# Attention with a pooled branch and top-128 routing: all stages placed anew in program order, pooling of q and k split over GpSimd and VectorE

## The chip, the cores and the metric

One core of one Trainium2 chip runs the whole program. The metric is device time in microseconds for one execution, the median of several runs. The engines are named as in the profile: PE is TensorE's matmul side and PEld its weight load, DVE is VectorE, ACT is ScalarE, POOL is GpSimd, and SP is the engine that only issues DMAs here.

## The reference, cut to what matters

Inputs are q, k and v with 8 batches, 8 heads, 576 rows and 64 columns. Two attentions are added. The coarse one averages q, k and v over groups of 4 rows (144 rows are left), does a full softmax attention on them, and repeats each result row 4 times. The local one is a softmax attention in which row i sees only the keys with |i - j| < 4. Their sum, with the heads side by side, is x (576 x 512 for each batch). Then a routed layer changes 128 rows of each batch:

```python
scores = np.einsum('bsd,d->bs', x, w_gate)
out = x.copy()
for b in range(B):
    top_idx = np.argpartition(-scores[b], capacity)[:capacity]   # capacity = 128
    xe = x[b, top_idx]
    h = np.maximum(xe @ w1, 0.0)                                  # w1 512 x 1024
    ye = h @ w2                                                   # w2 1024 x 512
    g = 1.0 / (1.0 + np.exp(-scores[b, top_idx]))
    out[b, top_idx] = x[b, top_idx] + g[:, None] * ye
```

## The kernel before, in words

All 8 batches are written out one after the other, and each is cut into generators ("stages"), whose steps are sorted by a position and run in that order to write the program. For batch b the stages are:

- QK (`load_qk`): two DMAs of 1152 KB from ACT's queue load q and k transposed into `T`, half of the head pairs each. Two buffers.
- PL (`pool_qk`): sums groups of 4 columns of `T` into `dT`, in four VectorE reductions of 128x1152 elements to 128x288 (L55 in the profile, where all DMAs and VectorE operations that go through the helper `InOrder` have that line). Two small ACT copies into `qz` follow.
- VP (`pool_v`): one DMA of 1152 KB loads `vraw`; three GpSimd additions of 128x576 make `vd` (L199, L201), and one multiplication makes `vr` (L205).
- VW (`load_vw`): three DMAs load windows of v for the local attention, with one buffer each (`vw0` to `vw2`).
- Two coarse units: scores `sd` (L229, L236), their maxima, exponentials `ed` (ACT, L254), transposes, and the products `od` (L295 to L308). Then ACT copies `odr` (L316), VectorE makes `ods` (L317), and SP issues DMAs that spread these rows four-fold into the tiles `x` (`raise_rows`, "x<-ods").
- Three local units (`sl`, `ex`, `pspl`, `pt`, `ol`, `t`) cover the five 116-row tiles; the first two units have two tiles each, the last has one. VectorE writes each tile's result `t` (L415).
- XS (`sums`), three steps: GpSimd adds `x = x + t` (L428), VectorE multiplies with the gate and sums into the score (`jk`, L430), SP writes `x` out.
- RT (`route`), 15 events: scores are compared all with all (`sb` L453, `srow` L455, five `beat` operations L466), the ranks give a one-hot matrix `oh`, a matmul `pi` (L487) gives the indices `idx` (L491). GpSimd issues the gather of the chosen rows (L498, `xe`). After six empty steps PE transposes them (`px`, L506), and ACT and VectorE split them into two fp16 parts (`xeh`, `xel`).
- MO (`moe`), 16 events: matmuls `ph` (L526 to L530) and `py` (L543 to L545), the final `xe` (L548), and GpSimd's scatter (L549).

Batch b's main units fill the position b to b + 1, in the proportions `WU`, each with three phases `PH`. Every other stage has a start and a span in `PLACE` against a base: b - 1 for QK, VP, VW and PL, b for XS, b + 1 for RT and MO; step i of n stands at base + start + span * (i + 0.5) / n. A last event also runs whatever steps its stage has left. Weights (WT) and constants (CS) are placed in the same way.

The sorted steps give the program's order. Three kinds of instructions keep that order strictly among themselves on their engine: DMAs and conversions on ACT called through `aq`, all of SP's DMAs, and the VectorE operations called through `vq` (pooling and weight conversion). For the rest the framework may let an instruction of the same engine pass ahead of one that is not ready by its own estimate. On the chip each engine runs its instructions strictly in the order it was given.

Of the kernel before, what the change touches and what calls it, by code (L numbers as in the profile page):

```python
# [11 lines left out]
F32 = mybir.dt.float32  # L12
# [4 lines left out]
ALU = mybir.AluOpType  # L17
AX = mybir.AxisListType
# [3 lines left out]
P = 128  # L22
# [11 lines left out]
XS = 16.0  # L34
WS = 64.0


PH = (-0.9, 0.2, 0.6)
WU = (2.2, 2.6, 5.2, 5.2, 2.6)
PLACE = {  # L40
# [4 lines left out]
}  # L45


# [11 lines left out]
def tile_multires_attention_moe(ctx: ExitStack, tc: tile.TileContext, qk, vw, vp, cs, w_gate, w1, w2, outs):  # L59


    nc = tc.nc
    B, _, _, HP, S = qk.shape
    pool = nc.gpsimd
    sp, aq, vq = (InOrder(tc, e) for e in (nc.sync, nc.scalar, nc.vector))
    D = P // 2
    H = 2 * HP
    DM = H * D
# [15 lines left out]
    ld = ctx.enter_context(tc.tile_pool(name="ld", bufs=2))  # L84
    wk = ctx.enter_context(tc.tile_pool(name="wk", bufs=2))
# [84 lines left out]
    def pool_qk(b):  # L170
        qkdT[b] = wk.tile([P, 2, HP, SD], F32, tag="dT", name=f"dT{b}")
        T, dT, hh = qkT[b], qkdT[b], HP // 2
        Tv = T.rearrange("p n h (c r) -> p n h c r", r=FACTOR)
        for u in range(2):
            hs = slice(hh * u, hh * (u + 1))
            for n in range(2):
                vq.tensor_reduce(out=dT[:, n, hs], in_=Tv[:, n, hs], axis=AX.X, op=ALU.add)
                yield
        qz = qzbuf[b % 2]
        for a in range(2):  # L180
            nc.scalar.copy(qz[64 * a : 64 * a + 64, :, a, :], dT[64 * a : 64 * a + 64, 0, :, P:])
        yield
# [158 lines left out]
    ts = [[] for _ in range(B)]  # L341
# [83 lines left out]
    def sums(b):  # L425
        for x, tiles in zip(xs, TU):
            for i, j in enumerate(tiles):
                pool.tensor_tensor(out=x[:, i], in0=x[:, i], in1=ts[b][j], op=ALU.add)  # L428
                jk = wk.tile([P, DM], F32, tag="jk", name="jk", bufs=1)
                nc.vector.scalar_tensor_tensor(  # L430
                    out=jk, in0=x[:, i], scalar=1.0, in1=wg, op0=ALU.mult, op1=ALU.mult,
                    accum_out=scs[b][:, j : j + 1],
                )
            for e in range(2):
                n = qns[2 * tiles[-1] + e]
                for p0, p1 in ((0, 48), (48, n)):
                    xv = bass.AP(
                        tensor=x_d[b].tensor, offset=x_d[b][2 * QB * tiles[0] + QB * e + p0, 0:1].offset,
                        ap=[[DM, p1 - p0], [2 * QB * DM, len(tiles)], [1, DM]],
                    )  # L440
                    sp.dma_start(out=xv, in_=x[64 * e + p0 : 64 * e + p1])
            yield


    def route(b, sc):
        va = vals[b % 2]
        scp = sm.tile([P, NT], F32, tag="scp", name="scp")
        nc.vector.tensor_tensor(out=scp, in0=sc, in1=pen, op=ALU.add)
        nc.scalar.copy(va[:, :, 1], scp)
        sb = psA.tile([P, 2, 512], F32, tag="A", name="sb")  # L450
        sbf = sb.rearrange("p a (j u) -> p (a j) u", u=P)
        for j in range(NT):
            nc.tensor.transpose(sbf[:, j], scp[:, j : j + 1].broadcast_to([P, P]), ident)  # L453
        srow = wk.tile([P, NT, P], F32, tag="srow", name="srow", bufs=2)
        nc.scalar.copy(srow, sbf[:, :NT])  # L455
        yield


        acc = sm.tile([P, NT], F32, tag="acc", name="acc")
        sr = srow.rearrange("p j u -> p (j u)")  # L460
        cb = psT.tile([P, 512], F32, tag="Q", name="cb")
        nc.tensor.matmul(cb[:, :NT], lhsT=identb, rhs=off, start=True, stop=False, skip_group_check=True)
        for j in range(NT):
            n = P * (NT - j)
            beat = wk.tile([P, NT, P], BF16, tag="beat", name="beat")
            nc.vector.scalar_tensor_tensor(  # L466
                out=beat[:, : NT - j].rearrange("p j u -> p (j u)"), in0=sr[:, P * j :],
                scalar=scp[:, j : j + 1], in1=first[:, :n], op0=ALU.subtract, op1=ALU.is_gt,
                accum_out=acc[:, j : j + 1],
            )  # L470
            for k in range(j + 1, NT):
                nc.tensor.matmul(
                    cb[:, k : k + 1], lhsT=beat[:, k - j], rhs=ones, start=False,
                    stop=j == NT - 2, skip_group_check=True,
                )
            yield
        nc.vector.scalar_tensor_tensor(
            out=acc, in0=acc, scalar=-1.0, in1=cb[:, :NT], op0=ALU.mult, op1=ALU.add
        )
        oh = wk.tile([P, NT, CAP], F32, tag="oh", name="oh", bufs=1)  # L480
        for j in range(NT):
            nc.scalar.activation(oh[:, j], iota, AF.Abs, bias=acc[:, j : j + 1])
        nc.scalar.activation(oh, oh, AF.Relu, bias=1.0, scale=-1.0)
        yield
        pi = psT.tile([P, 512], F32, tag="Q", name="pi")
        for j in range(NT):
            nc.tensor.matmul(  # L487
                pi[:, :2], lhsT=oh[:, j, :], rhs=va[:, j, :], start=j == 0, stop=j == NT - 1
            )
        idx = sm.tile([P, 1], I32, tag="idx", name="idx", bufs=3)  # L490
        nc.vector.tensor_copy(idx, pi[:, 0:1])  # L491
        gs = sm.tile([P, 1], F32, tag="gs", name="gs", bufs=3)
        nc.scalar.activation(gs, pi[:, 1:2], AF.Exp, scale=-1.0)
        nc.vector.tensor_scalar(gs, gs, 1.0, XS * WS * WS, op0=ALU.add, op1=ALU.mult)
        nc.vector.reciprocal(gs, gs)

        xe = wk.tile([P, DM], F32, tag="xe", name="xe", bufs=2)
        pool.indirect_dma_start(  # L498
            out=xe, out_offset=None, in_=x_d[b],
            in_offset=bass.IndirectOffsetOnAxis(ap=idx, axis=0),  # L500
        )
        for _ in range(6):
            yield
        px = psT.tile([P, NC, CAP], F32, tag="Q", name="px")
        for c in range(NC):
            nc.tensor.transpose(px[:, c, :], xe[:, P * c : P * (c + 1)], ident)  # L506
        xeh = wk.tile([P, NC, CAP], F16, tag="xeh", name="xeh", bufs=2)
        xel = wk.tile([P, NC, CAP], F16, tag="xel", name="xel", bufs=2)
        nc.scalar.activation(xeh, px, AF.Copy, scale=XS)  # L509
        nc.vector.scalar_tensor_tensor(  # L510
            out=xel, in0=px, scalar=XS, in1=xeh, op0=ALU.mult, op1=ALU.subtract
        )
        yield
        moes[b] = moe(b, idx, gs, xe, xeh, xel)
# [75 lines left out]

    ends = [sum(WU[:i]) / sum(WU) for i in range(len(WU) + 1)]
    nu = len(WU)
    mains = []
# [4 lines left out]
    for b in range(B):  # L598
        pq = put(lambda b=b: pool_qk(b), 5, *when("PL", b, b - 1), lqk[b])
        pv = put(lambda b=b: pool_v(b), 3, *when("VP", b, b - 1))  # L600
        lv = put(lambda b=b: load_vw(b), 3, *when("VW", b, b - 1))
        if weights is None:
            put(lambda: consts, 1, *when("CS", 0, -1))
            weights = put(load_weights, 11, *when("WT", 0, 0))
        for i in range(nu):
            need = (pq, pv) if i < 2 else ()
            g = put(lambda b=b, i=i: unit(b, i), 0, 0, 0, *need)
            e0, e1 = ends[i], ends[i + 1]
            for ph in range(3):
                events.append((b + e0 + PH[ph] * (e1 - e0), len(events), g, ph == 2))  # L610
            mains.append(g)
        xa = put(lambda b=b: sums(b), 3, *when("XS", b, b))
        rt = put(lambda b=b: route(b, scs[b]), 15, *when("RT", b, b + 1), *mains[-nu:], xa)
        put(lambda b=b: moes[b], 16, *when("MO", b, b + 1), weights, rt)
# [75 lines left out]
```

## Time and profile before

| | us |
|---|---|
| median of 3 runs | 398.24 |
| lowest, highest run | 394.81, 398.83 |
| the profiled execution | 392.69 |
| its span in the trace | 390.9 |
| mean granted TensorE clock in it | 0.847 of full speed |

All rows come from that one profiled execution, which is 1.4% shorter than the median; the 1.8 us outside its span are start and end of the program. A busy share is a mean over parts with different limits, so rows of one round (one batch's period) are read beside it. The chain of waits is followed back from the last instruction: at each step to what released it, or to the instruction before it on its engine.

### The profile page before, as it was taken

What the parts mean: (1) busy time and instruction counts of PE and PEld (TensorE: products, weight loads), DVE (VectorE), ACT (ScalarE), POOL (GpSimd) and SP (SyncE); (2) the same over time, 40 slices, a digit from 0 to 9 for tenths busy, and PEclk for the clock granted to TensorE, in tenths of its full rate; (3) what the DMA queues carried; (4) which work ended last, traced back from release to release, by engine and by line L of the source; (5) the groups of instructions that cost most, each with busy time, mean ns of one, the idle gap of its engine ahead of it and who ended that gap; (6) DMA issues with size and microseconds to landing.
All of it is one profiled execution on the core that took longest, in us unless ns stands there. A gap on an engine that the chain in (4) does not pass through costs nothing.

```text
span 390.9 us, 10860 instructions
## 1 busy us (share of the span) xinstructions
PE 297.6 (76%) x4584; PEld 224.3 (57%) x4584; DVE 250.8 (64%) x525; ACT 144.7 (37%) x385; POOL 117.9 (30%) x100
## 2 busy tenths in 40 slices
PE   0783568627999699849896699949996589985884
PEld 0553446526775686537665577637855467664471
DVE  2675978876677976565567877764675936576021
ACT  0543345623543353513534153513642144422210
POOL 3504620363008410652007510553009210251011
PEclk9996557956899899966999599966999569999599
DMA  8799877763578385845538375765567341642000
GB/s 314 284 329 291 266 224 282 209 170 61 196 270 194 90 261 197 200 147 174 198 109 229 95 251 171 216 169 150 173 231 176 87 118 29 130 104 74 27 29 27
DMA packets 24169, 67.93 MB, mean 174 GB/s; under 512 B 3608, under 2 KB 3736, under 8 KB 23096
## 3 DMA queue, kind: packets, MB, share of 16 engines
q10 hardware_dynamic: 10912, 43.55, 32.7%
q1 hardware_dynamic: 11928, 19.49, 21.3%
q0 software_dynamic: 1280, 4.20, 3.4%
q8 instruction: 36, 0.59, 0.6%
q14 instruction: 13, 0.11, 0.1%
HBM read 45.92 MB, written 11.53 MB: 147 GB/s over the span
## 4 chain that ended last, share of the span: by engine, by line
PE 32%; issue 17%; DVE 14%; POOL 13%; DMA 12%; ACT 7%; SPq 3%; POOLq 1%; ACTq 1%; DVEq 0%
POOL x L428 5%; DMA vraw<-in_vp_dram 5%; ACT ed L254 3%; POOL vd L201 3%; PE sd L229 3%; PE od L295 3%; SPq L55 3%; DVE jk L430 3%; DVE dT L55 3%; DMA x<-ods 3%; PE ph L526 3%; PE ph L529 2%; DMA out_dram<-x 2%; PE ph L530 2%; PE ol L405 2%
## 5 line engine op out<-in xcount | busy, mean ns | idle before, releaser
L428 POOL TENSOR_TENSOR x<-x,t 128x512 f32<-128x512 f32 x40 | 53.0, 1331 | 64.2 <-DVE t L415 44.1
L430 DVE SCALAR_TENSOR_TENSOR jk<-x,wg 128x512 f32<-128x512 f32 x40 | 38.9, 975 | 27.1 <-POOL x L428 25.4
L199 POOL TENSOR_TENSOR vd<-vraw 128x576 f32<-128x576 f32 x8 | 11.4, 1423 | 147.0 <-DMA vraw<-in_vp_dram 106.8
L529 PE MATMUL ph<-xel,w1h 128*128 128x128 f16 x256 | 49.9, 232 | 1.7 <-DVE xel L510 0.9
L526 PE MATMUL ph<-xeh,w1h 128*128 128x128 f16 x256 | 50.3, 233 | 0.7 <-ACT xeh L509 0.7
L530 PE MATMUL ph<-xeh,w1l 128*128 128x128 f16 x256 | 49.8, 232 | 0.0
L405 PE MATMUL ol<-vw,pt 64*64 64x65 f32 x1280 | 35.9, 257 | 17.8 <-DVE ex L383 4.6
L55 DVE TENSOR_REDUCE dT<-T 128x288 f32<-128x1152 f32 x32 | 42.8, 1343 | 4.1 <-DMA T<-in_qk_dram 4.1
L405 PEld LDWEIGHTS ol<-vw,pt 64*64 64x64 f32 x1280 | 29.3, 164 | 25.2 <-issue 13.8
L395 ACT COPY pt<-pspl 128x512 f32<-128x512 f32 x40 | 22.6, 585 | 32.6 <-PE pspl L393 32.5
L393 PE MATMUL pspl<-cst,ex 128*128 128x128 f32 x160 | 28.5, 318 | 6.9 <-ACT ex L387 6.2
L371 PE MATMUL sl<-T 64*58 64x64 f32 (+1 forms) x1280 | 32.2, 232 | 0.0
L371 PEld LDWEIGHTS sl<-T 64*58 64x58 f32 (+1 forms) x1280 | 27.8, 140 | 7.3 <-issue 5.7
L387 ACT ACTIVATE ex<-ex 128x1024 f32<-128x1024 f32 (+1 forms) x24 | 21.9, 913 | 26.5 <-DVE ex L383 26.5
L526 PEld LDWEIGHTS <-w1h 128*128 128x128 f16 x256 | 27.0, 106 | 4.1 <-issue 2.8
L415 DVE TENSOR_TENSOR t<-ol,den 128x512 f32<-128x512 f32 x40 | 27.6, 690 | 1.2
L529 PEld LDWEIGHTS <-w1h 128*128 128x128 f16 x256 | 27.0, 105 | 2.2 <-issue 1.6
L229 PE MATMUL sd<-dT 64*128 64x144 f32 x128 | 20.9, 434 | 9.5 <-DVE dT L55 7.9
L530 PEld LDWEIGHTS <-w1l 128*128 128x128 f16 x256 | 27.0, 106 | 1.6 <-issue 1.6
L380 DVE TENSOR_REDUCE mx<-sl 128x16 f32<-128x1024 f32 (+1 forms) x24 | 25.0, 1040 | 3.2 <-PE sl L371 3.2
L506 PE MATMUL px<-cst,xe 128*128 128x128 f32 x32 | 7.4, 375 | 25.2 <-DMA xe<-out_dram,idx 25.2
L254 ACT ACTIVATE ed<-sd,mxd 128x144 f32<-128x144 f32 x64 | 25.9, 525 | 0.5
(98 smaller groups left out, 604.3 us busy)
## 6 DMA issues: line engine op xcount, KB each, us to landing
T<-in_qk_dram ACTq DMA_DIRECT2D x16, 1152.0 KB
vraw<-in_vp_dram ACTq DMA_DIRECT2D x8, 1152.0 KB
vw<-in_vw_dram ACTq DMA_DIRECT2D x16, 520.0 KB
x<-ods SPq DMA_DIRECT2D x64, 120.0 KB
out_dram<-x SPq DMA_DIRECT2D x32, 192.0 KB
stg<-in_moe_w_dram ACTq DMA_DIRECT2D x8, 512.0 KB
vw<-in_vw_dram ACTq DMA_DIRECT2D x8, 260.0 KB
out_dram<-x SPq DMA_DIRECT2D x16, 96.0 KB
```

The source lines that it names most:

```text
L55: return lambda *a, **k: self.tc.keep_in_program_order(f(*a, **k))
L229: nc.tensor.matmul(s[:, a, SD * i : SD * (i + 1)], lhsT=dT[64 * a : 64 * a + 64, 0, hp, :P], rhs=dT[64 * a : 64 * a + 64, 1, hp, :], start ...
L254: nc.scalar.activation(ed[:, :, h] if h < H else er, s[:, a, SD * i : SD * (i + 1)], AF.Exp, bias=mx[:, c : c + 1], scale=pscale, accum_ou ...
L371: nc.tensor.matmul(s[64 * e : 64 * e + qn, a, c : c + KW], lhsT=T[64 * a : 64 * a + 64, 0, hp, q0s[blk] : q0s[blk] + qn], rhs=T[64 * a : 6 ...
L393: nc.tensor.transpose(ps[:, hp, :], ex[:, HP * i + hp, :], ident)
L405: nc.tensor.matmul(o[64 * e : 64 * e + 64, a, D1 * hp : D1 * (hp + 1)], lhsT=pt[64 * a : 64 * a + 64, hp, 64 * e : 64 * e + 64], rhs=vl[64 ...
L415: nc.vector.tensor_tensor(out=t.rearrange("p (g a d) -> p a g d", a=2, d=D), in0=ov[:, :, :, 0:D], in1=den.unsqueeze(3).broadcast_to([P, 2 ...
L428: pool.tensor_tensor(out=x[:, i], in0=x[:, i], in1=ts[b][j], op=ALU.add)
L430: nc.vector.scalar_tensor_tensor(out=jk, in0=x[:, i], scalar=1.0, in1=wg, op0=ALU.mult, op1=ALU.mult, accum_out=scs[b][:, j : j + 1],)
L526: nc.tensor.matmul(ph[:, i, :], lhsT=w1h[:, c, fs], rhs=xeh[:, c, :], start=c == 0, stop=False)
L529: nc.tensor.matmul(ph[:, i, :], lhsT=w1h[:, c, fs], rhs=xel[:, c, :], start=False, stop=False)
L530: nc.tensor.matmul(ph[:, i, :], lhsT=w1l[:, c, fs], rhs=xeh[:, c, :], start=False, stop=c == NC - 1)
```

## The change

Four things are changed.

1. Every number of `PH`, `WU` and `PLACE` is new, and so is the order of the program.
2. `pool_qk` does, for each half of the head pairs, one GpSimd addition of neighbouring columns (128x1152 results into a new tile `half`, two buffers, both inputs with stride 2) and, one step later, one VectorE addition of neighbouring results (128x576, both inputs with stride 2). The four reductions go.
3. In `sums`, the addition of `t` to `x` runs on VectorE for the last batch; for the others it stays on GpSimd. `jk` has two buffers.
4. `route` has eight empty steps in place of six after the gather, so that `px` falls on the stage's last event.

```diff
--- before.py
+++ after.py
@@ -35,13 +35,24 @@
 WS = 64.0
 
 
-PH = (-0.9, 0.2, 0.6)
-WU = (2.2, 2.6, 5.2, 5.2, 2.6)
+PH = (-0.9, 0.192, 0.601)
+WU = (2.19, 2.6, 5.16, 5.21, 2.548)
 PLACE = {
-    "QK": (-0.15, 0.2), "VP": (0.1, 0.7), "VW": (0.55, 0.75), "PL": (0.1, 0.7),
-    "RT": (0.0, 0.9), "MO": (0.8, 1.0), "CS": (0.6, 0.1), "XS": (0.45, 0.75), ("XS", 7): (0.3, 0.98), "WT": (0.0, 1.6),
-    ("RT", 7): (0.0, 0.5), ("MO", 5): (1.0, 0.9), ("MO", 6): (1.0, 0.5), ("MO", 7): (0.5, 0.5),
-    ("MO", 0): (1.0, 1.0),
+    "QK": (-0.164, 0.2),
+    "VP": (-0.041, 0.71),
+    "VW": (0.292, 0.507),
+    "PL": (0.084, 0.717),
+    "RT": (0.0, 0.936),
+    "MO": (0.971, 0.985),
+    "CS": (0.54, 0.212),
+    "XS": (0.472, 0.839),
+    ("XS", 7): (0.268, 1.075),
+    "WT": (-0.173, 1.567),
+    ("RT", 7): (-0.027, 0.719),
+    ("MO", 5): (0.548, 1.14),
+    ("MO", 6): (1.077, 0.52),
+    ("MO", 7): (0.988, 0.487),
+    ("MO", 0): (1.04, 0.905),
 }
 
 
@@ -173,9 +184,13 @@
         Tv = T.rearrange("p n h (c r) -> p n h c r", r=FACTOR)
         for u in range(2):
             hs = slice(hh * u, hh * (u + 1))
-            for n in range(2):
-                vq.tensor_reduce(out=dT[:, n, hs], in_=Tv[:, n, hs], axis=AX.X, op=ALU.add)
-                yield
+            hv = ld.tile([P, 2, hh, S // 2], F32, tag="half", name="half", bufs=2)
+            e2 = T.rearrange("p n h (c r) -> p n h c r", r=2)
+            pool.tensor_tensor(out=hv, in0=e2[:, :, hs, :, 0], in1=e2[:, :, hs, :, 1], op=ALU.add)
+            yield
+            h2 = hv.rearrange("p n h (c r) -> p n h c r", r=2)
+            vq.tensor_tensor(out=dT[:, :, hs], in0=h2[..., 0], in1=h2[..., 1], op=ALU.add)
+            yield
         qz = qzbuf[b % 2]
         for a in range(2):
             nc.scalar.copy(qz[64 * a : 64 * a + 64, :, a, :], dT[64 * a : 64 * a + 64, 0, :, P:])
@@ -425,8 +440,9 @@
     def sums(b):
         for x, tiles in zip(xs, TU):
             for i, j in enumerate(tiles):
-                pool.tensor_tensor(out=x[:, i], in0=x[:, i], in1=ts[b][j], op=ALU.add)
-                jk = wk.tile([P, DM], F32, tag="jk", name="jk", bufs=1)
+                last = b == B - 1
+                (nc.vector if last else pool).tensor_tensor(out=x[:, i], in0=x[:, i], in1=ts[b][j], op=ALU.add)
+                jk = wk.tile([P, DM], F32, tag="jk", name="jk", bufs=2)
                 nc.vector.scalar_tensor_tensor(
                     out=jk, in0=x[:, i], scalar=1.0, in1=wg, op0=ALU.mult, op1=ALU.mult,
                     accum_out=scs[b][:, j : j + 1],
@@ -499,7 +515,7 @@
             out=xe, out_offset=None, in_=x_d[b],
             in_offset=bass.IndirectOffsetOnAxis(ap=idx, axis=0),
         )
-        for _ in range(6):
+        for _ in range(8):
             yield
         px = psT.tile([P, NC, CAP], F32, tag="Q", name="px")
         for c in range(NC):
```

## Rows read from the trace of the kernel before

**Rows 1.** Busy time, share of the span and instruction count of each engine (the page's first part), whole span.
```profile
PE 297.6 (76%) x4584; PEld 224.3 (57%) x4584; DVE 250.8 (64%) x525; ACT 144.7 (37%) x385; POOL 117.9 (30%) x100
```

**Rows 2.** Busy time of each engine in five stretches, each from the end of one batch's `od` matmuls (L308) to the next one's (the first begins earlier, at 100.0, inside batch 2's round). Columns: start:end and length in us; busy us and instructions of PE, PEld, DVE, ACT, POOL; granted TensorE clock as a share of full speed; DMA share; GB/s. The last row has sum and mean.
```profile
100.00:152.40 52.40, 47.73 (x816) 37.41 (x811) 40.37 (x85) 23.32 (x66) 14.33 (x11) 0.96 0.65 200
152.40:200.80 48.40, 39.77 (x563) 29.32 (x562) 28.93 (x66) 17.14 (x47) 13.95 (x11) 0.86 0.56 163
200.80:241.30 40.50, 33.23 (x576) 26.28 (x574) 31.23 (x62) 16.93 (x47) 13.46 (x11) 0.87 0.65 194
241.30:286.40 45.10, 38.73 (x585) 29.07 (x583) 28.42 (x64) 17.00 (x47) 14.03 (x11) 0.85 0.60 175
286.40:330.50 44.10, 34.47 (x548) 25.96 (x546) 29.23 (x64) 16.36 (x46) 13.47 (x11) 0.81 0.47 125
sum 230.50, PE 193.93 PEld 148.04 DVE 158.18 ACT 90.75 POOL 69.24; mean PE 38.79 PEld 29.61 DVE 31.64 ACT 18.15 POOL 13.85
```

**Rows 3.** The chain that ended last over the whole span, in order of time: start us, us, what (a row with "DMA" runs from issue to landing); first its shares by line.
```profile
by line: issue 17.4%; POOL x L428 5.0%; DMA vraw<-in_vp_dram 5.0%; ACT ed L254 3.4%; POOL vd L201 3.1%; PE sd L229 3.0%; PE od L295 3.0%; SPq L55 2.9%; DVE jk L430 2.8%; DVE dT L55 2.8%; DMA x<-ods 2.7%; PE ph L526 2.6%; PE ph L529 2.4%; DM
...
1.43 8.43 DMA T<-in_qk_dram
...
25.69 8.27 DMA vraw<-in_vp_dram
...
84.99 4.47 issue
...
152.38 0.87 PE od L308 x2
153.35 5.84 DMA vraw<-in_vp_dram
...
200.83 0.87 PE od L308 x2
...
206.67 3.02 DMA x<-ods
...
217.77 4.50 issue
...
241.34 0.87 PE od L308 x2
242.31 5.53 DMA vraw<-in_vp_dram
...
286.40 0.87 PE od L308 x2
...
295.38 3.50 DMA x<-ods
...
303.33 5.48 issue
...
330.52 0.86 PE od L308 x2
```

**Rows 4.** Timeline of POOL from 195 to 345 us (batches 4 and 7): start us, us, engine, line, operation, out<-in, count, and in brackets the idle time before it and what ended that.
```profile
207.53 1.44 POOL L199 TENSOR_TENSOR vd<-vraw 128x576 f32<-128x576 f32 x1 [23.26 <-DMA vraw<-in_vp_dram]
...
211.95 0.98 POOL L498 DMA_INDIRECT xe<-out_dram,idx  x1 [0.30 <-issue]
...
214.30 2.48 POOL L428 TENSOR_TENSOR x<-x,t 128x512 f32<-128x512 f32 x2
216.73 1.04 POOL L205 TENSOR_TENSOR vr<-vd,cst 128x512 f32<-128x512 f32 x1
...
340.99 1.27 POOL L428 TENSOR_TENSOR x<-x,t 128x512 f32<-128x512 f32 x1 [1.88 <-issue]
```

**Rows 5.** Timeline of DVE from 195 to 232 us, same columns.
```profile
207.88 0.16 DVE L491 CAST idx<-pi 128x1 int32<-128x1 f32 x1 [0.17 <-PE pi L487]
...
215.60 2.73 DVE L430 SCALAR_TENSOR_TENSOR jk<-x,wg 128x512 f32<-128x512 f32 x1 [2.88 <-POOL x L428]
```

**Rows 6.** Waits between 60 and 345 us, one row: engine and line that waited, what it waited for, us in total, times, longest.
```profile
PE px L506 <- DMA xe<-out_dram,idx: 25.2, 6, 6.3
```

**Rows 7.** Timeline of PE from 205 to 226 us, same columns.
```profile
217.92 1.08 PE L506 MATMUL px<-cst,xe 128*128 128x128 f32 x4 [4.90 <-DMA xe<-out_dram,idx]
...
219.09 1.15 PE L405 MATMUL ol<-vw,pt 64*64 64x65 f32 x32
...
225.44 0.70 PE L405 MATMUL ol<-vw,pt 64*64 64x65 f32 x32
```

**Rows 8.** Groups of instructions by line and shape over the whole span: xcount | busy us, mean ns of one | idle before, with what ended it.
```profile
L428 POOL TENSOR_TENSOR x<-x,t 128x512 f32<-128x512 f32 x40 | 53.0, 1331 | 64.2 <-DVE t L415 44.1 <-DVE den L413 13.8 <-DMA out_dram<-x 4.5
...
L55 DVE TENSOR_REDUCE dT<-T 128x288 f32<-128x1152 f32 x32 | 42.8, 1343 | 4.1 <-DMA T<-in_qk_dram 4.1
L430 DVE SCALAR_TENSOR_TENSOR jk<-x,wg 128x512 f32<-128x512 f32 x40 | 38.9, 975 | 27.1 <-POOL x L428 25.4 <-DMA out_dram<-x 1.4 <-DMA x<-ods 0.3
...
L201 POOL TENSOR_TENSOR vd<-vd,vraw 128x576 f32<-128x576 f32 x16 | 24.3, 1520 | 0.9
```

**Rows 9.** Timeline of all engines from 353.2 to 356.3 us (the last tile of the last batch), same columns as the other timelines.
```profile
353.33 0.69 DVE L415 TENSOR_TENSOR t<-ol,den 128x512 f32<-128x512 f32 x1
...
354.15 1.27 POOL L428 TENSOR_TENSOR x<-x,t 128x512 f32<-128x512 f32 x1 [1.91 <-DVE t L415]
...
355.46 0.69 DVE L430 SCALAR_TENSOR_TENSOR jk<-x,wg 128x512 f32<-128x512 f32 x1 [0.84 <-POOL x L428]
```

## The prediction

> **What bounds the kernel now.** I read the busy shares first: no engine is full, PE is busy 76% of the span, DVE 64%, POOL 30% [rows 1]. So the time is made of waits between engines, and the next view is the stretches of one batch each. The chain of waits passes the end of `od` at 153.25, 201.70, 242.21, 287.26 and 331.38 us [rows 3], so a round takes (331.38 - 153.25) / 4 = 44.5 us, of which PE is busy 33 to 40, DVE 28 to 31 and POOL 14 [rows 2]. Third, the chain itself. In these rounds it runs from the end of `od` into the DMA of `vraw` (5.84 and 5.53 us, 8.27 in the first round), through POOL's three `vd` additions, the gather and the `x` additions, and then into stretches marked "issue" of 4.47, 4.50 and 5.48 us [rows 3]. The timelines explain both pieces for batch 4. `vraw` is issued from ACT's queue behind the copy of `od`, so it starts only when `od` ends; POOL sits idle for 23.26 us until it lands, and everything behind it in POOL's queue starts late: the gather at 211.95, though its indices were there at 208.04 [rows 4, 5], and the first `x` addition at 214.30, 12.6 us after `od`. PE then reaches `px` at 213.0 and stands still for 4.90 us until the gathered rows land [rows 7]. That idle time also costs clock: right after it the 32 `ol` matmuls take 1.15 us, as at 1.2 GHz, against 0.70 us later at 2.4 GHz [rows 7]; the granted clock was 0.81 to 0.87 in the four full rounds and 0.96 in the stretch before [rows 2].
>
> **The change part by part.** Positions are in rounds.
>
> *(a) VP earlier.* `vraw` moves from 0.217 to 0.077 of a round, ahead of the coarse unit's second and third phases (0.152 and 0.212), so its DMA no longer waits for `od`; its additions move from 0.45 to 0.314. The wait of [rows 4] goes. What is late next is seen in batch 7, which has no `vraw` behind it: its first `x` addition starts at 340.99, 9.6 us after `od` [rows 3, 4]; the spread rows land at 206.67 + 3.02 = 209.69, 8.0 us after `od`. Gain per round: 12.6 - 9.6 = 3.0, at least 0, at most 12.6 - 8.0 = 4.6. Six rounds: -18.0 (0 to -27.6).
>
> *(b) Gather to `px`.* The gather stands at 0.468 (before 0.45), `px` on RT's last event at 0.905 (before 0.81), so the distance grows from 0.36 to 0.437 of a round, 3.4 us more. Before, PE came to `px` 5.0 us after the indices (213.02 against 208.04) and the gather needed 217.92 - 211.95 = 6.0 us after 3.9 us of delay on POOL. After, PE comes 8.4 us behind the indices, and the gather needs 6.0, or 8.7 if it stands behind the new second GpSimd addition (0.442): a wait of 0 to 0.3 us. PE's six waits are 25.2 us in all [rows 6]; only the three "issue" pieces on the chain count, 14.5 [rows 3]. Against that, batch 5's new MO start (0.548) pulls its `px` forward to 0.116 after the gather, about 5 us, where one wait like the old ones returns (4.5). Sum -10.0 (-25.2 to +4.5).
>
> *(c) Pooling.* Removed: 32 reductions of 1.343 us, 43.0 us of DVE [rows 8]. Added on DVE: 16 additions of 576 elements. Nearest is `jk`, also two SBUF operands: 0.69 us for 512 undisturbed [rows 9], so 0.75 (up to 2.73, its longest [rows 5]); 12.0 in all. Added on POOL: 16 additions of 1152. The `x` addition takes 1.27 us for 512 undisturbed [rows 4, 9], which makes 2.9 for 1152; `vr` takes 1.04 for 512, which makes 2.3; the mean of `vd` is 1.52 for 576, which makes 3.0 [rows 4, 8]. I take 2.7 (2.3 to 3.0; stride 2 on GpSimd is in no row): 43 us, 5.4 a round on an engine that is busy 14 of 44.5. That hides them, and the DVE half is one step (0.143 round, 6.4 us) later, so it does not wait. On the chain the reductions have 2.8% of 390.9 = 10.9 us [rows 3]; shortened in the ratio 12/43 that leaves 3.0: -7.9 (0 to -10.9). The other side is a collision. A DVE operation with two SBUF operands does not run beside a POOL addition: `jk` began at 215.60 and lasted 2.73 us, until the POOL operations then running (`x` to 216.78, `vr` to 217.77) were over [rows 4, 5]. In the mean `jk` takes 0.975 against 0.69 [rows 8, 9], so 40 x 0.285 = 11.4 us are lost beside 117.9 us of POOL. POOL becomes 117.9 + 43 - 6.7 (five `x` additions gone) = 154, which makes the loss 14.9, and 16 new DVE additions are exposed by 0.285 each, 4.6: +8 on DVE, half of it on the chain: +4 (0 to 16 x 2.7 = 43). Together -3.9.
>
> The Trainium skill speaks against this part: "GPSIMD Engine Reference", § 4.1 Engine selection, sends elementwise work on a tile to VectorE and calls GpSimd about twice as slow for two inputs, and § 1 Specifications says its SBUF interfaces are shared with VectorE where that has two SBUF inputs. The 2.73 us row agrees with the second. By the first rule alone the kernel would get slower by this part; the third rival below is that case.
>
> *(d) `x` on DVE for batch 7.* Last tile: `t` ends at 354.02, `jk` begins at 355.46 after the POOL addition [rows 9], 1.44 us; DVE's own addition takes about 0.69. -0.75, and the same for the tile before: -1.5 (-2 to +2.1, if the three other additions fall on the path). The rest of the tail keeps its order: `ph` of batch 6 before the routing, `py` behind `pi`, then `px`.
>
> *(e) Start.* Earlier issue of the first round's `vraw` (8.27 us on the chain) by 0.14 round would be worth 6, but five weight loads now stand ahead of position 0.47 instead of three and share the DMA engines: -2. The price the other way: batch 0's second GpSimd addition is placed behind `vd`, so if it runs there, pooling ends 3 x 1.4 + 2.7 = 7 us later. Range -6 to +7.
>
> *Loads with one buffer.* The `vw` loads now stand before the last reader of their buffer (0.377 against 0.446 and so on), so they go out when it is free, and the next `T` loads queue behind the last of them, at about 0.95 instead of 0.90. `T` is needed at 1.156, 9 us later; a `T` load took 8.43 in the crowded start [rows 3], so 0, up to +2 a round. The second `jk` buffer changes nothing: DVE writes them in order.
>
> *The other places.* The `x` steps move from 0.575 and 0.825 to 0.612 and 0.891, with the output DMAs that SP issues for them; the last step stays at 1.03, and SP's next work, the spread of the next batch, stands at 1.21, 8 us later, so SP has time. MO moves back by 0.16 of a round, its scatter on POOL from 0.519 to 0.679, behind the first `x` additions instead of ahead of them; only the program's end waits for a scatter. These are costed at nothing; if the later `x` steps reach the spread, they cost what they moved, 0.05 round or 2 us each round.
>
> Sum: -18.0 - 10.0 - 3.9 - 1.5 - 2.0 = -35.4. PE would allow it: busy time times clock is 31.0 us a round in the four full rounds; at clock 0.96 and the 91% share of the first stretch (47.73 of 52.40) a round needs 35.5 us, below the 44.5 - 5.3 = 39.2 of the sum. But (a), (b) and (c) lie on one chain with PE, DVE and SP close behind, so I count two thirds of their 31.9: -21. With (d) and (e): -24.5, 392.7 to 368.2. The runs' median is 398.24 / 392.69 = 1.014 of the profiled execution, so 373.4; I say 373.
>
> **Rivals.**
> 1. *The whole sum.* -35.4: 357.3, in the median's measure 362. For it: the 35.5 us that PE needs. Against: rounds without a `vraw` or `px` piece on the chain are not shown.
> 2. *The next wait takes its place.* SP's spread DMAs, on the chain with 3.02 and 3.50 us just before `x`, end last anyway; then (a) and (c) are worth nothing, (b) half (-5), and (d) and (e) stay: -8.5, 384.2, so 390.
> 3. *POOL's additions become the wall.* Each of the 16 additions stops a two-operand DVE operation for its full 2.7 us and holds the gather and the `x` behind it: +43, (a) lost, (b) half: -5, reductions -7.9, (d) and (e) -3.5: +27, 420, so 425. It decides once about 10 of the 16 stops fall on the chain (24.5 / 2.7, and (a) lost with them). Against: POOL is idle 30 of 44.5 us a round, and the positions lie away from `jk`.
> 4. *The order is not what the positions say.* The framework lets ready instructions pass, and the engines' order hardly differs: within 1%, 398.
>
> **How the numbers follow.** Forecast 0.50, rivals 0.18, 0.15, 0.11 and 0.06. The forecast's own range is 365 to 385. Low end 358, below the whole sum; high end 398, which leaves out rival 3 and little else. A measurement here tells about 1% from no change (394.3 to 402.2). Faster: 0.49 + 0.18 + 0.12 = 0.79; same: 0.01 + 0.03 + 0.05 = 0.09; slower: the rest, 0.12.
>
> **What would show it.** Right: POOL's long idle before `vd` no longer ends with `vraw`'s DMA on the chain; the first `x` starts under 10 us after `od`; PE's waits at `px` fall from 25.2 us to 5; the granted clock in the rounds rises to 0.9 or more; the GpSimd additions take 2.7 us and DVE's 0.75; a round is near 41 us. Wrong: `jk` and `beat` longer in the mean than now, DVE idle ended by POOL's additions, or the chain passing through SP's spread DMAs in every round, with rounds of 44 us.

## The result: 365.0 us, and where the time went

The changed kernel takes 365.0 us (median of 4 runs, 363.12 to 375.13); the kernel before, run beside it, 397.41 (394.81 to 398.83). The ratio is 0.9176, 95% interval [0.9101, 0.9251]. The profiled execution takes 364.34 us with a span of 362.5, against 392.69 and 390.9: -28.3 us, where the prediction counted -24.5 of a sum of -35.4. Some executions of a kernel take over 1.5% longer than its fastest one; the ratios leave them out, none is given where only one execution is left (e1, e12 below), and the profiles of e1, e10 and e12 are of such executions. From L55 on, all lines stand 11 to 16 further down in the new program (L55 is L66, `od`'s end L323, `x` L444, `jk` L446, `beat` L482, gather L514, `px` L522, scatter L565).

Busy time of each engine over the span (answers [rows 1]):
```profile
PE 289.3 (80%) x4584; PEld 215.6 (59%) x4584; DVE 253.1 (70%) x514; ACT 143.1 (39%) x385; POOL 151.8 (42%) x111
```
VectorE is as busy as before, 253.1 us against 250.8, though 32 reductions of 1.34 us became 16 additions: the first surprise.

Five rounds, each from the end of one batch's `od` to the next one's; columns as in [rows 2], which this answers:
```profile
113.50:151.40 37.90, 35.22 (x613) 26.68 (x612) 30.68 (x63) 16.36 (x47) 20.23 (x15) 1.00 0.70 209
151.40:189.70 38.30, 34.59 (x575) 25.93 (x574) 30.80 (x63) 16.46 (x47) 19.73 (x14) 0.96 0.69 205
189.70:227.60 37.90, 34.45 (x576) 26.07 (x575) 30.97 (x64) 16.58 (x47) 19.46 (x14) 0.95 0.70 208
227.60:263.80 36.20, 33.21 (x576) 24.80 (x575) 27.79 (x61) 16.49 (x47) 16.95 (x12) 1.00 0.73 217
263.80:306.90 43.10, 39.01 (x573) 27.84 (x572) 27.63 (x64) 17.39 (x48) 12.67 (x11) 0.96 0.43 107
```
The first four of these are the rounds of batches 2 to 6, and they hold nearly all of the gain. In one stretch each, first before, then after:
```profile
112.40:287.30 174.90, 148.50 (x2331) 113.20 (x2334) 120.53 (x257) 68.39 (x190) 55.77 (x44) 0.88 0.61 180
```
```profile
113.50:263.80 150.30, 137.47 (x2332) 103.49 (x2331) 120.24 (x249) 65.89 (x188) 76.37 (x53) 0.98 0.71 210
```
That is -24.6 us. The rest of the span: up to the first `od` +2.5 (25.6 to 28.1), the two rounds after it -1.4, the last round -1.0, the tail behind the last `od` -3.9 (59.5 to 55.6); together -28.4. A middle round was 43.7 us, PE busy 37.1 and idle 6.6, at clock 0.88; now it is 37.6, busy 34.4 and idle 3.2, at 0.98. So a little over half of the gain is idle time of PE that went (3.4 a round), and the rest is the same matmuls (2331 and 2332) taking 2.8 us less at the higher clock.

The chain of waits, cut to one round (answers [rows 3]):
```profile
by line: issue 13.5%; DMA xe<-out_dram,idx 8.6%; SPq L66 8.1%; DVE beat L482 7.9%; DMA x<-ods 5.4%; DMA T<-in_qk_dram 4.9%; DMA vw<-in_vw_dram 3.6%; ACT ed L269 3.1%; PE ol L420 2.4%; DMA stg<-in_moe_w_dram 2.2%; DVE jk L446 1.9%; PE sl L38
...
226.76 0.86 PE od L323 x2
228.98 0.89 SPq L66
...
231.72 3.39 DMA x<-ods
235.14 6.66 DMA xe<-out_dram,idx
243.23 6.57 DMA vw<-in_vw_dram
```
`vraw` is gone from it. On the chain now are SP's spread, then the gather, which `px` waits for. POOL in that round (answers [rows 4]):
```profile
217.32 4.75 POOL L189 TENSOR_TENSOR half<-T 128x1152 f32<-128x1152 f32 x2 [5.23 <-DMA out_dram<-x]
222.78 1.41 POOL L214 TENSOR_TENSOR vd<-vraw 128x576 f32<-128x576 f32 x1 [0.70 <-DMA vraw<-in_vp_dram]
224.26 3.13 POOL L216 TENSOR_TENSOR vd<-vd,vraw 128x576 f32<-128x576 f32 x2
227.77 1.04 POOL L220 TENSOR_TENSOR vr<-vd,cst 128x512 f32<-128x512 f32 x1 [0.37 <-PE od L323]
233.73 1.27 POOL L444 TENSOR_TENSOR x<-x,t 128x512 f32<-128x512 f32 x1 [4.92 <-DMA x<-ods]
235.14 1.34 POOL L514 DMA_INDIRECT xe<-out_dram,idx  x1
```
The `vd` additions stand before the end of `od` (227.6), where they stood behind it; their wait for `vraw` falls from 23.3 us at the longest to 4.8. The first `x` starts 6.1 us after `od`; in batches 1 to 6 it starts 6.1 to 7.7 us after, against 8.6 to 12.6 before. The bracket names the spread, but in this round `x` waits for `t` as much: VectorE's `t` ends at 233.65, and `x` starts 0.08 us later.
```profile
232.96 0.69 DVE L430 TENSOR_TENSOR t<-ol,den 128x512 f32<-128x512 f32 x1
```

PE's wait at `px` (answers [rows 6]), and PE at that place (answers [rows 7]):
```profile
PE px L522 <- DMA xe<-out_dram,idx: 11.7, 6, 3.5
```
```profile
239.80 0.58 PE L420 MATMUL ol<-vw,pt 64*64 64x65 f32 x28
241.85 0.66 PE L522 MATMUL px<-cst,xe 128*128 128x128 f32 x4 [1.46 <-DMA xe<-out_dram,idx]
...
242.44 0.70 PE L420 MATMUL ol<-vw,pt 64*64 64x65 f32 x32
```
The wait is there still, in six rounds, but it is short, and the 32 `ol` behind it take 0.70 us, the speed of 2.4 GHz.

Groups by shape (answers [rows 8]), and VectorE in batch 7's last tiles (answers [rows 9]):
```profile
L446 DVE SCALAR_TENSOR_TENSOR jk<-x,wg 128x512 f32<-128x512 f32 x40 | 32.6, 817 | 16.0 <-POOL x L444 14.2 <-DMA T<-in_qk_dram 1.4 <-DMA out_dram<-x 0.3
...
L66 DVE TENSOR_TENSOR dT<-half 128x576 f32<-128x576 f32 x16 | 18.8, 1182 | 7.6 <-POOL half L189 7.6
L482 DVE SCALAR_TENSOR_TENSOR beat<-srow,scp,first 128x512 bf16<-128x512 f32 x8 | 13.3, 1664 | 0.0
...
L189 POOL TENSOR_TENSOR half<-T 128x1152 f32<-128x1152 f32 x16 | 35.7, 2252 | 45.2 <-DMA T<-in_qk_dram 35.2 <-DMA out_dram<-x 9.9
```
```profile
322.60 0.69 DVE L430 TENSOR_TENSOR t<-ol,den 128x512 f32<-128x512 f32 x1
323.33 0.69 DVE L444 TENSOR_TENSOR x<-x,t 128x512 f32<-128x512 f32 x1
324.06 0.69 DVE L446 SCALAR_TENSOR_TENSOR jk<-x,wg 128x512 f32<-128x512 f32 x1
```

### The profile page after: what moved, and what is told of

Read it like the earlier page. It is cut to its first block, busy times and chain, and to the rows that moved or that the text cites. A ratio compares the mean times of both kernels' runs of the same rounds, so it can differ in the third digit from the quotient of the medians.

```text
span 362.5 us, 10864 instructions
## 1 busy us (share of the span) xinstructions
PE 289.3 (80%) x4584; PEld 215.6 (59%) x4584; DVE 253.1 (70%) x514; ACT 143.1 (39%) x385; POOL 151.8 (42%) x111
## 4 chain that ended last, share of the span: by engine, by line
DMA 25%; PE 22%; DVE 18%; issue 13%; SPq 8%; ACT 7%; POOL 4%; ACTq 1%; POOLq 0%; DVEq 0%
DMA xe<-out_dram,idx 9%; SPq L66 8%; DVE beat L482 8%; DMA x<-ods 5%; DMA T<-in_qk_dram 5%; DMA vw<-in_vw_dram 4%; ACT ed L269 3%; PE ol L420 2%; DMA stg<-in_moe_w_dram 2%; DVE jk L446 2%; PE sl L386 2%; PE od L310 2%; DVE mxd L257 2%; PE ph L542 1%; DVE dT L66 1%
## 5 line engine op out<-in xcount | busy, mean ns | idle before, releaser
L444 POOL TENSOR_TENSOR x<-x,t 128x512 f32<-128x512 f32 x35 | 46.8, 1342 | 82.3 <-DVE t L430 40.2
L189 POOL TENSOR_TENSOR half<-T 128x1152 f32<-128x1152 f32 x16 | 35.7, 2252 | 45.2 <-DMA T<-in_qk_dram 35.2
L482 DVE SCALAR_TENSOR_TENSOR beat<-srow,scp,first 128x640 bf16<-128x640 f32 (+4 forms) x40 | 46.8, 1207 | 1.2 <-ACT srow L471 0.7
L446 DVE SCALAR_TENSOR_TENSOR jk<-x,wg 128x512 f32<-128x512 f32 x40 | 32.6, 817 | 16.0 <-POOL x L444 14.2
L420 PE MATMUL ol<-vw,pt 64*64 64x65 f32 x1280 | 29.7, 234 | 14.7 <-DVE ex L398 7.5
L420 PEld LDWEIGHTS ol<-vw,pt 64*64 64x64 f32 x1280 | 24.5, 144 | 21.5 <-issue 10.6
L386 PE MATMUL sl<-T 64*58 64x64 f32 (+1 forms) x1280 | 34.4, 230 | 0.0
L430 DVE TENSOR_TENSOR t<-ol,den 128x512 f32<-128x512 f32 x40 | 27.6, 691 | 1.3
L408 PE MATMUL pspl<-cst,ex 128*128 128x128 f32 x160 | 26.0, 300 | 1.5 <-ACT ex L402 1.5
L546 PEld LDWEIGHTS <-w1l 128*128 128x128 f16 x256 | 26.6, 104 | 0.7 <-issue 0.6
L216 POOL TENSOR_TENSOR vd<-vd,vraw 128x576 f32<-128x576 f32 x16 | 26.3, 1647 | 1.2
L514 POOL DMA_INDIRECT xe<-out_dram,idx x8 | 10.1, 1260 | 38.8 <-DVE idx L507 22.1
```

The lines of the kernel that those rows point to most:

```text
L189: pool.tensor_tensor(out=hv, in0=e2[:, :, hs, :, 0], in1=e2[:, :, hs, :, 1], op=ALU.add)
L386: nc.tensor.matmul(s[64 * e : 64 * e + qn, a, c : c + KW], lhsT=T[64 * a : 64 * a + 64, 0, hp, q0s[blk] : q0s[blk] + qn], rhs=T[64 * a : 6 ...
L420: nc.tensor.matmul(o[64 * e : 64 * e + 64, a, D1 * hp : D1 * (hp + 1)], lhsT=pt[64 * a : 64 * a + 64, hp, 64 * e : 64 * e + 64], rhs=vl[64 ...
L430: nc.vector.tensor_tensor(out=t.rearrange("p (g a d) -> p a g d", a=2, d=D), in0=ov[:, :, :, 0:D], in1=den.unsqueeze(3).broadcast_to([P, 2 ...
L444: (nc.vector if last else pool).tensor_tensor(out=x[:, i], in0=x[:, i], in1=ts[b][j], op=ALU.add)
L446: nc.vector.scalar_tensor_tensor(out=jk, in0=x[:, i], scalar=1.0, in1=wg, op0=ALU.mult, op1=ALU.mult, accum_out=scs[b][:, j : j + 1],)
```

## The experiments

Theory A: the places did it, above all VP's (`vraw` off the chain) and the longer way from gather to `px`. Rival B: the lighter VectorE did it, by the pooling. Theory C came up after the first kernels: QK's place, because it takes the `T` loads past other work on ACT's queue. Each part was undone in the new kernel, or done alone in the old one. All of them in one table; the kernel before took 395.68, 394.9 and 397.13 us beside the three groups (e1, e2, e3, e5; e10, e11, e12, e4; e13, e6, e14, e15). "Round" is the mean of the four middle rounds of the profile, as PE's busy plus idle time, from one stretch as above.

| kernel | median us | ratio [95%] | round | clock |
|---|---|---|---|---|
| the change | 365.0 | 0.9176 [0.9101, 0.9251] | 34.4 + 3.2 | 0.98 |
| e1 change, pooling undone | 361.57 | none given; 361.57/395.68 = 0.914 | 34.7 + 3.3 | 0.98 |
| e2 before + pooling | 395.09 | 0.9991 [0.9944, 1.0039] | 36.2 + 6.5 | 0.90 |
| e3 before + VP | 391.75 | 0.9874 [0.9757, 0.999] | 37.0 + 5.5 | 0.91 |
| e5 change, VP undone | 388.47 | 0.9813 [0.9731, 0.9895] | 36.0 + 6.0 | 0.93 |
| e10 change, QK undone | 363.22 | 0.9136 [0.9051, 0.9222] | 35.4 + 3.4 | 0.96 |
| e11 before + VP, QK | 376.79 | 0.9495 [0.9428, 0.9562] | 34.9 + 5.5 | 0.94 |
| e12 before + VP, QK, RT, MO | 380.37 | none given; 380.37/394.9 = 0.963 | 37.4 + 5.9 | 0.90 |
| e4 before + RT, MO | 407.35 | 1.0269 [1.0198, 1.0341] | 37.2 + 6.3 | 0.90 |
| e13 change, RT, MO undone | 380.3 | 0.9606 [0.954, 0.9672] | 35.5 + 3.8 | 0.95 |
| e6 change, `x` on GpSimd | 368.65 | 0.928 [0.9211, 0.9349] | 35.2 + 4.0 | 0.96 |
| e14 change, VW, XS undone | 361.17 | 0.9137 [0.9062, 0.9213] | 35.0 + 2.5 | 0.97 |
| e15 before + VP, QK, VW, XS | 382.91 | 0.9654 [0.9573, 0.9735] | 36.6 + 4.9 | 0.93 |

**The pooling: e1 and e2.** The changed kernel with the four reductions a batch, and the old one with the two pairs of additions.
```diff
 e1, against the changed kernel (e2 is the reverse, against the kernel before)
-            hv = ld.tile([P, 2, hh, S // 2], F32, tag="half", name="half", bufs=2)
-            e2 = T.rearrange("p n h (c r) -> p n h c r", r=2)
-            pool.tensor_tensor(out=hv, in0=e2[:, :, hs, :, 0], in1=e2[:, :, hs, :, 1], op=ALU.add)
-            yield
-            h2 = hv.rearrange("p n h (c r) -> p n h c r", r=2)
-            vq.tensor_tensor(out=dT[:, :, hs], in0=h2[..., 0], in1=h2[..., 1], op=ALU.add)
-            yield
+            for n in range(2):
+                vq.tensor_reduce(out=dT[:, n, hs], in_=Tv[:, n, hs], axis=AX.X, op=ALU.add)
+                yield
```


> The changed kernel with the four VectorE reductions of the kernel before in pool_qk, at the changed kernel's places. Theory A (the new places make the gain; the reductions saved on VectorE come back as beat and jk operations stretched beside GpSimd's additions, so pooling is worth little): 361 to 370 us, beat back from 1.21 to 0.61 us in the mean. Rival B (the gain is the 31 us less pooling work on VectorE): 380 us or more.

> The kernel before with only the new pooling (one GpSimd and one VectorE addition for each half). Theory A: 392 to 404 us, with beat and jk stretched beside GpSimd. Rival B: 383 us or less.

e1 (355.7 to 364.35 us) takes no more time than the change (363.12 to 375.13), if anything less, and e2 no less than the kernel before, though VectorE's busy time in e2 is 26.6 us a round against 30.1. Rival B is out: the whole gain is there without the pooling, and on the old order a lighter VectorE brings nothing. Of e1 one part was missed: `beat`'s total stays at 38.6 us (22.9 in the kernel before, 46.8 in the changed one). By shape in e1:
```profile
L478 DVE SCALAR_TENSOR_TENSOR beat<-srow,scp,first 128x256 bf16<-128x256 f32 x8 | 9.5, 1186 | 0.0
...
L478 DVE SCALAR_TENSOR_TENSOR beat<-srow,scp,first 128x512 bf16<-128x512 f32 x8 | 6.0, 748 | 0.0
```
Without `half` the 512 form is back at 0.748 us (1.664 in the changed kernel), but the forms behind it are not: with VP early they stand beside the `vd` additions. In e1 the first `od` ends at 25.1 us; in the changed kernel at 28.1.

**VP's place: e3 and e5.**
```diff
 e3, against the kernel before (e5 is the reverse, against the changed kernel)
-    "VP": (0.1, 0.7),
+    "VP": (-0.041, 0.71),
```


> The kernel before with only the new place of VP (vraw issued at 0.077 of a round in place of 0.217). By the prediction's step (a) the six rounds lose 3.0 us each: 378 to 384 us, the first x addition under 10 us after od, and the px wait shrinks as the gather leaves POOL earlier. Rival B: 394 us or more.

> The changed kernel with VP back at its old place. Theory A with step (a): 378 us or more, POOL idle before vd until vraw lands, again behind od. If VP's place is worth little beside the other places: 364 to 369 us. Rival B: 366 us.

Undone in the new kernel, VP costs 0.9813 - 0.9176 = 6.4%, some 25 us, in every round (41.1 to 42.7 in the middle): behind the later `vd`, the first `x` starts 8.9 to 10.8 us after `od` in batches 2 to 5 and the gather 10.3 to 12.2, where the change has 6.1 to 7.0 and 7.5 to 8.4. Done alone in the old one it gives 1.3%, 5 us, with an interval that nearly reaches no change: A's number for e3 was missed. POOL in e3, batch 3, whose `od` ends at 156.5, and VectorE beside it show what came last once `vraw` did not:
```profile
165.18 1.02 POOL L549 DMA_INDIRECT out_dram<-xe,idx  x1 [6.46 <-DVE xe L548]
166.51 0.98 POOL L498 DMA_INDIRECT xe<-out_dram,idx  x1 [0.30 <-issue]
169.35 2.50 POOL L428 TENSOR_TENSOR x<-x,t 128x512 f32<-128x512 f32 x2 [1.85 <-DVE den L413]
```
```profile
165.16 0.16 DVE L491 CAST idx<-pi 128x1 int32<-128x1 f32 x1 [0.26 <-PE pi L487]
...
168.57 0.69 DVE L415 TENSOR_TENSOR t<-ol,den 128x512 f32<-128x512 f32 x1
```
An earlier batch's scatter waits 6.46 us for its expert rows, with the gather queued behind it. But the gather's indices end only at 165.32, so that cost it 1.2 us, and `x` waits 1.85 us more, for VectorE's `t`, which ends at 169.26. In all six rounds of e3 the first `x` starts within 0.1 us behind the end of `t`, 7.5 to 12.9 us after `od`. With `vraw` out of the way the next wait was `t`, which VP does not move; so VP pays only with what else moved.

**QK's place: e10 and e11.** QK's shift is 0.014 of a round; `T`'s loads then stand at 0.886 and 0.986, ahead of ACT's coarse exponentials (0.889 and 0.992) on the queue that issues them.
```diff
 e10, against the changed kernel
-    "QK": (-0.164, 0.2),
+    "QK": (-0.15, 0.2),
 e11, against the kernel before
-    "QK": (-0.15, 0.2), "VP": (0.1, 0.7), ...
+    "QK": (-0.164, 0.2), "VP": (-0.041, 0.71), ...
```


> The changed kernel with QK back at its old place (0.90 and 1.00 of a round in place of 0.886 and 0.986), so that each T load stands on ACT's queue behind a coarse unit's exponentials (0.889 and 0.992) in place of ahead of them. Theory C (the T loads must leave early so that vraw has the DMA engines for itself; VP's place works only with it): T is issued some 10 us later in the round, vraw lands beside it, 378 to 390 us. Theory D (0.014 of a round is nothing): 363 to 367 us.

> The kernel before with the new places of VP and QK only. Theory C: 376 to 386 us, vraw landed before od ends, the px wait still there. Theory D: as with VP alone, 390 to 393 us.

On the old order the shift is worth 391.75 - 376.79 = 15 us beside VP. ACT's queue in e11, batch 4, 21.9 and 27.6 us after `od` (190.6):
```profile
212.50 0.55 ACTq L55 DMA_DIRECT2D T<-in_qk_dram  x1
217.49 0.52 ACT L254 ACTIVATE ed<-sd,mxd 128x144 f32<-128x144 f32 x1
...
218.21 0.79 ACTq L55 DMA_DIRECT2D T<-in_qk_dram  x1
```
In the kernel before these two go out 24.9 and 32.2 us after `od` (226.64 and 233.92, `od` at 201.70). But in the new kernel the old place costs nothing (e10: 363.22), though `T` goes out 3 to 15 us later there, counted from `od`. C's number came on the old order and failed on the new. Its reason is not seen in either: the first `vd` addition, which waits for `vraw`, starts no earlier in e11 (3.2 us before the end of `od` to 0.5 after it, in batches 2 to 6) than in e3 (3.4 before to 0.2 after). What the 15 us are stays open.

**Gather to `px`, RT and MO: e4, e12 and e13.**
```diff
 e4, against the kernel before (e12: with e11's edits; e13: the reverse, against the changed kernel)
-    "RT": (0.0, 0.9), "MO": (0.8, 1.0), ... ("MO", 0): (1.0, 1.0),
+    "RT": (0.0, 0.936), "MO": (0.971, 0.985), ... ("MO", 0): (1.04, 0.905),
...
-        for _ in range(6):
+        for _ in range(8):
             yield
```


> The kernel before with only RT's and MO's new places and the eight empty steps (px at 0.905 in place of 0.81). By the prediction's step (b): 384 to 390 us, PE's waits at px from 25 us to under 8. If vraw's wait decides alone: 393 to 399 us, with the px waits gone all the same.

> The kernel before with the new places of VP and QK, of RT and MO (but for MO of batches 5 to 7 and RT of batch 7), and eight empty steps after the gather. Theory C with the px wait as the third part: 364 to 372 us, the whole gain without pooling on GpSimd. If the other places (VW, XS, WU, PH) are needed: 376 us or more.

> The changed kernel with RT and MO at their old places (but for MO of batches 5 to 7 and RT of batch 7) and six empty steps, so px is back at 0.81 and the gather at 0.45. If step (b) holds once vraw is out of the way: 370 us or more, PE's px waits above the changed kernel's 11.7 us. If the later px is worth nothing, as the run with only these places suggests: 362 to 368 us.

Alone the edit makes the kernel slower by 2.7%, 11 us, while PE's waits at `px` fall from 25.2 to 11.0 us. The loss lies in one round, batch 1 to 2, and 4.6 us in the tail (64.1 against 59.5):
```profile
69.80:123.40 53.60, 36.34 (x539) 28.77 (x539) 32.42 (x65) 19.23 (x49) 13.85 (x10) 0.71 0.51 142
```
against 43.50 us at clock 0.76 in the kernel before. In e12 no `px` waits in the middle rounds, and its executions, 374.39 to 381.03 us and well above what was expected, are not faster than e11's (375.48 to 379.91), which has 12.9 us of such waits there. Both edits move MO as well, so they do not price the wait alone; but no gain came with its going. Yet undoing the same edit in the new kernel (e13) costs 0.9606 - 0.9176 = 4.3%, 17 us, with `px` waits of 14.7 us against 11.7: they can't be the reason. e13's rounds from batch 2 on are 35.8, 39.8, 45.5, 36.1 and 46.5 us: some as short as the change's, some as long as before. POOL in e13, batch 4, whose `od` ends at 190.9:
```profile
201.54 1.27 POOL L444 TENSOR_TENSOR x<-x,t 128x512 f32<-128x512 f32 x1 [5.72 <-DVE t L430]
202.97 1.35 POOL L565 DMA_INDIRECT out_dram<-xe,idx  x1 [0.16 <-issue]
204.63 0.98 POOL L514 DMA_INDIRECT xe<-out_dram,idx  x1 [0.30 <-DMA x<-odr]
205.63 1.27 POOL L444 TENSOR_TENSOR x<-x,t 128x512 f32<-128x512 f32 x1
```
`x` is back at 10.7 to 11.1 us after `od` in batches 3 to 6, and what it waits 5.72 us for is `t`. PE's order shows why `t` and the indices are late: MO's matmuls `py` of an earlier batch stand ahead of the local unit's `ol` and of the routing's `pi`.
```profile
194.05 0.38 PE L559 MATMUL py<-w2h,hh 128*128 128x512 f16 x1
...
198.44 0.38 PE L561 MATMUL py<-w2h,hl 128*128 128x512 f16 x1
198.75 0.57 PE L420 MATMUL ol<-vw,pt 64*64 64x65 f32 x20
...
201.31 1.18 PE L503 MATMUL pi<-vals,oh 128*128 128x2 f32 x10
```
```profile
200.77 0.69 DVE L430 TENSOR_TENSOR t<-ol,den 128x512 f32<-128x512 f32 x1
```
In the changed kernel (batch 5, whose `od` ends at 227.6) `py` stands behind both:
```profile
230.53 0.70 PE L420 MATMUL ol<-vw,pt 64*64 64x65 f32 x32
231.15 1.28 PE L503 MATMUL pi<-vals,oh 128*128 128x2 f32 x10
232.29 0.38 PE L559 MATMUL py<-w2h,hh 128*128 128x512 f16 x1
```
There `t` ends 6.0 us after `od` and the indices 6.1; in e13's batch 4 it is 10.6 and 12.6. The short rounds of e13 are the two whose indices end 6.2 and 6.7 us after `od`, the long ones have them at 11.4 to 12.7; `t` alone does not decide, it ends at 11.0 in the short round of batch 5. The scatter is ahead of the gather again, but the gather starts 1.1 us behind its indices, so little of the time is there. That MO's matmuls make the 17 us is read from these rows: they were not moved without RT, so it is argued, not shown.

**`x` for the last batch: e6.**
```diff
-                last = b == B - 1
+                last = False
```


> The changed kernel with the last batch's x additions back on GpSimd. By step (d): 1.5 us more, 365 to 368, the time from the last batch's od to the end about 57 us in place of 55.6. If DVE's own additions were on the path as long as GpSimd's: no difference.

The tail behind the last `od` is 57.7 us against 55.6: 2.1 us for the five additions. Each is from one profile. The other rounds, which this edit doesn't touch, differ too: the four middle ones are 6.5 us longer together, the ones around them 4.6 shorter. The two intervals overlap, so the times alone show no difference.

**VW and XS: e14 and e15.**
```diff
 e14, against the changed kernel (e15: the reverse edit, on e11)
-    "VW": (0.292, 0.507),
-    "XS": (0.472, 0.839),
-    ("XS", 7): (0.268, 1.075),
+    "VW": (0.55, 0.75),
+    "XS": (0.45, 0.75),
+    ("XS", 7): (0.3, 0.98),
```


> The changed kernel with VW and XS at their old places. If these two are what the kernel with VP and QK alone (377 us) lacks: 373 to 380 us, rounds of 39.5 us or more in place of 38.0. If the rest lies in other places: 362 to 368 us.

> The kernel before with the new places of VP, QK, VW and XS. If VW and XS are the rest: 364 to 370 us. If not: 374 to 380 us, as with VP and QK alone.

These places add nothing: without them the new kernel is at 361.17 (its interval overlaps the change's), and with them e11 goes from 376.79 to 382.91, another miss. In e14 no `px` waits in the middle rounds and PE is idle only 2.5 us:
```profile
112.90:262.60 149.70, 139.84 (x2361) 106.19 (x2360) 112.58 (x251) 65.82 (x188) 78.11 (x54) 0.97 0.72 211
```

**What stays open.** From the old side the best set of parts reached 377 us (e11), from the new side 361 to 363 us remain with pooling, QK, or VW and XS undone, for the change's 365. What makes up these 12 to 16 us was not told apart: the edit of RT and MO in company with PH, WU, PL, CS, WT and the special places of MO 5 to 7, RT 7. The parts don't add up: VP is worth 5 or 25 us, QK 15 or 0, RT and MO -11 or +17, by what stands around them.

## Why the prediction was right, and where it was not

**What bounds the kernel: right.** Waits between engines were the time, PE's clock followed its idle time, and the new order shortened the round until PE is busy 91% of it: 34.4 of 37.6 us is the share that the prediction took for its floor, at clock 0.98, not 0.96. That PE now bounds the round is not shown: the chain of waits passes through it for 22% of the span. The forecast of a round near 41 us was too long by 3, and the gain, -24.5 for -28.3, too small.

**(a) VP: the right place, mis-sized, and not alone.** In the six rounds `x` came 1.6 to 6.5 us earlier, 4.5 in the mean, against 3.0, which was read from the longest of them; in three it was 5.2 or more, beyond the 4.6 set as the most it could give. That bound took the landing of the spread on the chain, which is a later one of several; in the new trace `x` starts at 233.73, and the spread on the chain lands at 231.72 + 3.39 = 235.11, so the first `x` needs only an earlier one. And the step held only in company: 18 us stood in the sum for VP by itself, where e3 measured 5 and e5 25. What the step left out is the other input of `x`. The prediction named the spread as what is late next, but its own row for that, batch 7's `x` at 340.99, stands 0.14 us behind the end of `t`, and in e3 and e13 `x` waits for `t`:
```profile
340.16 0.69 DVE L415 TENSOR_TENSOR t<-ol,den 128x512 f32<-128x512 f32 x1
```

**(b) Gather to `px`: wrong.** Forecast: waits of 0 to 0.3 us, 10 us gained. Measured: six waits of 0.7 to 3.5, 11.7 in all. PE came to `px` 6.7 us behind the indices, not 8.4 (240.4 against 233.73), and the gather needed 6.66, not 6.0, after 1.4 us behind the first `x` addition. Only batch 5 came out as argued, 3.5 against 4.5. The price of the wait was the worse mistake: in e4 and e12 most or all of it goes and nothing is gained on the old order, and on the new one e14, where `px` doesn't wait in the middle rounds, is not measurably faster either. A chain of waits shows one wait as the last; it does not show how near the next is.

**(c) Pooling: near nothing, by two errors of size.** Forecast -3.9, of which two thirds were counted; e2 measures nothing, e1 nothing or a small loss. The GpSimd addition takes 2.25 us in the mean (2.10 at the shortest), below the 2.7 taken and below its lower bound of 2.3, which came from `vr`. The VectorE addition takes 0.75 undisturbed (the median), as forecast, but 1.18 in the mean. The collision was counted as +8 us of VectorE, and on the old order it was that: undisturbed, VectorE should save 42.8 - 12.0 = 30.8 us, and in e2 it is 23.8 us less busy (227.0 for 250.8), so 7.0 were lost. In the new order it is near +24: with the pooling VectorE is busy 253.1 us, without it (e1) 259.6, a saving of 6.5. `beat` rises most, from 22.9 to 46.8 us, but e1 has 38.6 of them without the pooling; that part goes to the `vd` additions, which stand beside it in the new order. The prediction looked at `jk` alone, which became shorter (0.975 to 0.817), and took the mean exposure of the old places for the new ones. VectorE beside POOL's `half` of 217.32 to 222.07 and `vd` behind it:
```profile
218.11 2.00 DVE L482 SCALAR_TENSOR_TENSOR beat<-srow,scp,first 128x640 bf16<-128x640 f32 x1 [0.69 <-ACT srow L471]
...
220.04 2.58 DVE L482 SCALAR_TENSOR_TENSOR beat<-srow,scp,first 128x512 bf16<-128x512 f32 x1
```
The Trainium skill, "GPSIMD Engine Reference", § 1 Specifications, says that VectorE with two SBUF inputs contends with GpSimd for the SBUF interfaces; the trace agrees, with 2.58 us for 0.75. By the Trainium skill, "GPSIMD Engine Reference", § 4.1 Engine selection, GpSimd is about twice as slow for two inputs; here `x` takes 1.27 us there and 0.69 on VectorE. As a verdict on the whole part the rule went too far: the kernel did not get measurably slower by it.

**(d) `x` on VectorE: right.** From `t`'s end to `jk` 0.77 us (323.29 to 324.06) for 1.44; 2.1 us by e6's profile, 1.5 forecast.

**(e) The start: the wrong sign.** +2.5 us for -2, inside its range. The two first `half` additions ran at 9.91 to 14.07 us, ahead of `vd` and not behind it; e1, with reductions, has its first `od` 3.0 us earlier, and e2, with the pooling on the old order, 2.8 us later than the kernel before (28.4 for 25.6), so it is the pooling that costs here.

**Places costed at nothing: the gap.** MO's move stood in the prediction as without a price, because only the program's end waits for a scatter. That looked at MO's last instruction. Its matmuls stand in PE's queue, at the old place ahead of `ol` and `pi` (e13), where some 5 us of `py` hold up `t` and the indices; undoing RT and MO cost 17 us. QK's move had no term of its own, and `T`, forecast to go out later, goes out earlier (15.2 us after `od` in batch 4, 24.9 before). The total came near by luck: what (b) did not bring, (a) in company and the places without a term did.

**The rivals.** The whole sum, 362, is nearer to the 365.0 measured than the forecast of 373, but its terms did not come as they were summed. The next wait did take its place: the spread is on the chain of every round but one, the gather on that of most. But they end so much earlier that the rounds are short. POOL's wall did not come: POOL is busy 151.8 us (154 forecast) and the kernel is faster. The order did change.

## What to carry to other kernels

Where a stall at the head of an in-order queue goes, list what stands next in that queue and what each of these waits for, on every input: here `x` needed the spread and `t`, and `t` hung on what PE had to do first. The wait on the chain is only the last of several. When a stage moves, look at all its instructions on every engine, not only at the last one. Undo each part in the new kernel as well as doing it alone in the old one: here the same edit was worth 25 us from one side and 5 from the other, another 17 and -11, and each number alone would have told a false story. An addition moved from VectorE to GpSimd is paid by whichever two-operand VectorE work stands beside it, so read that from the new order, not from the mean of the old.

## What the runs showed of the hardware

Where two-operand VectorE work stood beside two GpSimd additions, both got longer: a `beat` took 2.58 us for 0.75, and the second of the two additions 2.69 for 2.10 (the two are the row of 4.75 us). Over the kernel the pooling additions cost VectorE some 24 us in the new order and 7 in the old. The stride-2 GpSimd addition was no slower than a plain one: 2.10 us for 1152 elements at the shortest, 1.8 ns each, against 1.27 us for 512, 2.5 ns each. And a shift of 0.014 of a round, past the exponentials on the queue that issues a load, moved the time by 15 us in one order and by nothing in another.
